# A linear-attention block and a gated mixture of experts on one core: routing steps that read and write PSUM, and another order of the first loads and tables

## Chip, cores and metric

The kernel runs on one core of a Trainium2 chip. The metric is the device time of one execution in microseconds, the median of several runs. Engines are named as in the profile: PE (TensorE), DVE (VectorE), ACT (ScalarE), POOL (GpSimd), SP (the engine that only issues DMAs here); ACT and POOL issue DMAs as well.

## The reference

Linear attention with a state (4 batches, 8 heads, 768 positions, head size 48), and then a mixture of experts with two levels of gates on the 3072 resulting rows of 384 (4 groups of 4 experts, hidden size 1024), all in float32:

```python
for t in range(S):                                  # attention
    cur = einsum('bhd,bhe->bhde', u * k[t], v[t])
    y[t] = einsum('bhd,bhde->bhe', r[t], state + cur)
    state = w * state + einsum('bhd,bhe->bhde', k[t], v[t])
...
g_logits = x @ w_group                              # 4 groups, argmax and softmax weight
e_logits = x @ w_expert[g]                          # 4 experts of that group, the same
out[row] = g_w * e_w * (relu(x[row] @ w1[g, e]) @ w2[g, e])
```

## The kernel before

The positions are cut into 6 chunks of 128, so that there are 24 tiles (chunk, batch). A loop written out by hand over `s` in 0 to 28 (line 510) works on several tiles at once, in this order within a step: `turn(s)` transposes r and k and scales r with a power table (`rT`, line 402; `kT`, copied by ACT, line 404); `own_values(s-1)` (ACT, eight small scalings `dv`); the routing part `choice` if one is due; `rows_T(s-4)` and `row_logits(s-5)` transpose the finished rows and multiply them with the gate weights; `back(s-3)` turns the output back (`xt`, line 471); `values(s-2)` multiplies the masked scores with v (`py`) and updates the state (`pu`, then `R`, lines 455 to 459); `own_sum` (`du`, line 383); the routing parts that are due last; and `scores(s-1)` (`pa`, line 414), which DVE masks into `am` (line 419). The order of each engine's instructions is this program order.

POOL computes `kh` (k times a table, line 373) and `dg` (r times k times u, lines 378 and 379) for pairs of tiles; both multiply 768 elements per partition with both operands in SBUF. It also sends the finished rows to their places in DRAM (`rows`, line 331), with an indirect DMA each.

Routing is done for groups of tiles: five groups of four, then one of two and two of one. `choice` (lines 284 to 297) is due one step after the group's last logits, `gate` and `place` (lines 310 to 327) another step later, `before` ahead of them. All of these are short DVE instructions on tiles in SBUF; the logits are copied from PSUM to `lg` by ACT (line 362). `zero_places` (line 260) clears the rows' places in DRAM in two pieces, from the ACT queue. All PSUM tiles come from one pool of eight banks (line 74).

In the head, `w` is loaded to `w2h` and scanned into powers (`up_to`). Three tables `T1T` (`powers`, line 177) and, turned and flipped by PE and copied by ACT, three tables `T2` (`turned`, line 183) are made from them. `powers(2)`, `turned(0)`, `powers(0)` come ahead of the loop; `later_tables` (line 237) does the rest in step 1. A copy by ACT into `none` (line 156) comes ahead of the scan, and DVE rewrites that column (line 157). All loads of r, k and v (384 KB each) go out on the SP queue; `u` (`ub`), `w` (`wrow`) and the gate weights (`gw`) on the ACT queue.

Behind the loop, the 16 experts run one after the other: `load_rows`, `columns` (transposes), `up` (`ph`, line 632), `down` (`po`, line 645), `rows_out` (line 650). Each expert fills two `px`, four `ph`, three `po` and two `pb` banks.

Of the kernel before, what the change touches and what calls it, by code (L numbers as in the profile page):

```python
# [8 lines left out]
FP32 = mybir.dt.float32  # L9
# [3 lines left out]
OP = mybir.AluOpType  # L13
# [15 lines left out]
def kernel(  # L29
# [43 lines left out]
    wpool = ctx.enter_context(tc.tile_pool(name="wpool", bufs=1))  # L73
    psum = ctx.enter_context(tc.tile_pool(name="psum", bufs=8, space=bass.MemoryType.PSUM))

    def bank(shape, name):
        return psum.tile(shape, FP32, tag="bank", name=name)

    def cst(shape, name, dtype=FP32):
        return const.tile(shape, dtype, name=name)  # L80
# [34 lines left out]

    def load(src, g, dst):
        c, b0 = g // (B // 2), 2 * (g % (B // 2))
        nc.sync.dma_start(
            out=dst.rearrange("p a h d -> p (a h) d"),
            in_=src[b0 : b0 + 2, :, P * c : P * (c + 1), :].rearrange("b h t d -> t (b h) d"),  # L120
        )

    def load_pair(g):

        load(r, g, rts[g % RING][:, :, :, 0:D])
        load(k, g, kts[g % RING])
        load(v, g, vts[g % (RING + 1)][:, :, :, 0:D])

    ub = cst([P, H, D], "ub")
    nc.scalar.dma_start(  # L130
        out=ub.rearrange("p h d -> p (h d)"), in_=bass.AP(tensor=u.tensor, offset=u.offset, ap=[[0, P], [1, H * D]])
    )
    wrow = cst([1, H * D], "wrow")
    nc.scalar.dma_start(out=wrow, in_=bass.AP(tensor=w.tensor, offset=w.offset, ap=[[0, 1], [1, H * D]]))
    load_pair(0)

# [40 lines left out]
    def powers(m):  # L177
        for hc in range(HP):
            nc.vector.tensor_scalar(
                out=T1T[m][:, hc, :], in0=up_to[:, hc, :], scalar1=by[:, m, hc : hc + 1], scalar2=None, op0=OP.mult  # L180
            )

    def turned(m):

        ptab = bank([P, HP, P], "ptab")
        for hc in range(HP):
            nc.tensor.transpose(ptab[:, hc, :], T1T[SPAN - 1 - m][:, hc, :], ident)
        tab = cst([P, HP, P], f"tab_{m}")
        nc.scalar.copy(tab, ptab)
        ptab2 = bank([P, HP, P], "ptab2")  # L190
        nc.tensor.matmul(
            ptab2.rearrange("p a b -> p (a b)"), lhsT=flip, rhs=tab.rearrange("p a b -> p (a b)"), start=True, stop=True
        )
        nc.scalar.copy(  # L194
            T2[m].rearrange("p (a e) d -> p a e d", e=2), ptab2.rearrange("p a (e d) -> p a e d", e=2)[:, :, :, 0:D]
        )
# [4 lines left out]
    nc.vector.tensor_mul(by[:, 0, :], by[:, 0, :], by[:, 1, :])  # L201
    powers(0)


# [31 lines left out]

    def later_tables():
        powers(1)
        turned(1)
        turned(2)  # L240
        nc.vector.tensor_mul(w_span, up_to[:, :, P - 1], up_to[:, :, P - 1])
        nc.vector.tensor_mul(w_span, w_span, up_to[:, :, P - 1])
# [17 lines left out]
    def zero_places(j):  # L260

        regions = xs_dram.rearrange("(e n) w -> n e w", e=GE)
        half = CAP // 2
        nc.scalar.dma_start(out=regions[half * j : half * (j + 1)], in_=spread(nothing[0:half, :], 1, GE))

    def route(pool, lg, xt, T, sums, number, group):

# [5 lines left out]

        NA = 1 + G
        L = lg.rearrange("p i (a e) -> p i a e", e=Eg)
        mx, kx = tl([P, T, NA], "mx"), tl([P, T, NA], "kx")
        key, oh = tl([P, T, NA, Eg], "key"), tl([P, T, NA, Eg], "oh")
        ohe = tl([P, T, G, Eg], "ohe")
        ohf = ohe.rearrange("p i g e -> p i (g e)")
        ex = tl([P, T, NA, Eg], "ex")  # L280
# [3 lines left out]
        def choice():  # L284
            nc.vector.reduce_max(out=mx, in_=L, axis=AX)  # L285

            nc.vector.tensor_tensor(out=key, in0=L, in1=spread(mx, 3, Eg), op=OP.is_ge)
            nc.vector.tensor_mul(
                key.rearrange("p i a e -> p (i a) e"), key.rearrange("p i a e -> p (i a) e"), spread(desc, 1, T * NA)
            )  # L290
            nc.vector.reduce_max(out=kx, in_=key, axis=AX)
            nc.vector.tensor_tensor(out=oh, in0=key, in1=spread(kx, 3, Eg), op=OP.is_equal)
            nc.vector.tensor_mul(ohe, oh[:, :, 1:NA, :], spread(oh[:, :, 0, :], 3, Eg))
            for i in range(T):
                nc.vector.tensor_add(sums[:, i + 1, :], sums[:, i, :], ohf[:, i, :])
            nc.vector.tensor_sub(ex, L, spread(mx, 3, Eg))
            nc.scalar.activation(ex, ex, AF.Exp)
# [12 lines left out]
        def gate():  # L310
            sx = tl([P, T, NA], "sx")
            nc.vector.reduce_sum(out=sx, in_=ex, axis=AX)
            nc.vector.tensor_scalar(out=sx, in0=sx, scalar1=1e-9, scalar2=None, op0=OP.add)
            gg = tl([P, T, G], "gg")
            nc.vector.tensor_mul(gg, sx[:, :, 1:NA], oh[:, :, 0, :])
            se = tl([P, T], "se")
            nc.vector.reduce_sum(out=se, in_=gg, axis=AX)
            nc.vector.tensor_mul(se, se, sx[:, :, 0])
            nc.vector.reciprocal(xt[:, :, DM + ROW_GATE], se)
            nc.vector.tensor_copy(xt[:, :, DM + ROW_ID], number)  # L320

        def place():
            at = tl([P, T, GE], "at")
            nc.vector.tensor_mul(at, held["pre"], ohf)  # L324
            place = tl([P, T], "place")
            nc.vector.reduce_sum(out=place, in_=at, axis=AX)
            nc.vector.tensor_copy(place_i, place)

# [28 lines left out]

    def logits(xT, dst):
        pl = bank([P, NL], "pl")
        for ko in range(KO):  # L360
            nc.tensor.matmul(pl, lhsT=xT[:, ko, :], rhs=gw[:, ko, :], start=(ko == 0), stop=(ko == KO - 1))
        nc.scalar.copy(dst, pl)

# [57 lines left out]
    def values(n):  # L421
# [29 lines left out]
        for e in range(2):  # L451
            rows = slice(DP * e, DP * (e + 1))
            state = R[b][rows, :, DP * e : DP * e + D]
            if c == 0:
                nc.vector.tensor_copy(state, pu[rows])
            else:
                nc.vector.tensor_add(state, pu[rows], state)
            if c % SPAN == SPAN - 1:
                nc.vector.tensor_mul(state, state, spread(w_span[rows, :], 2, D))

    def back(n):

        c, b = tiles[n]
        yT = yTs.pop(n)
        if b == 0:
            xts[c] = pool.tile([P, B, XW], FP32, tag="xt", bufs=3, name="xt")
            lgs[c] = pool.tile([P, B, NL], FP32, tag="lg", bufs=3, name="lg")
        pb = bank([P, HP, 2, DP], "pb")
        for hc in range(HP):
            nc.tensor.transpose(pb[:, hc].rearrange("p e d -> p (e d)"), yT[:, hc, :], ident)  # L470
        nc.vector.tensor_add(
            xts[c][:, b, 0:DM].rearrange("p (h d) -> p h d", h=H), pb.rearrange("p a e d -> p (a e) d")[:, :, 0:D],
            dvs.pop((n // 2, n % 2)),
        )
# [5 lines left out]

    def row_logits(n):
        c, b = tiles[n]
        logits(xTs.pop(n), lgs[c][:, b, :])


    ROUTED = {B * c + B - 1: B for c in range(NCH - 1)}
    ROUTED.update({NT - 3: 2, NT - 2: 1, NT - 1: 1})

    def routing(n):
        T = ROUTED[n]  # L490
        c, b = tiles[n]
        first = n + 1 - T
        b0 = b + 1 - T
        return route(
            rpool, lgs[c][:, b0 : b + 1, :], xts[c][:, b0 : b + 1, :], T, cum[:, first : n + 2, :],
            tok[:, c, b0 : b + 1], "rows to places",
        )
# [3 lines left out]
    scale_k(0, nc.gpsimd, 1, 2)  # L501
    for t in rts[1:] + khs[1:] + vts[1:]:
        nc.gpsimd.memset(t[:, :, :, D:DP], 0.0)
    load_small()
    load_pair(1)
    own(0)
# [3 lines left out]
    for s in range(NT + LAST):  # L510
# [11 lines left out]
        if s % 2 == 0 and s // 2 + 2 < NP:  # L522
            load_pair(s // 2 + 2)
        if s in (3, 6):
            zero_places(s // 6)
        if s == 18:
            early[0] = load_expert(0, wpool)
        run("first")
        if s < NT:
            turn(s)  # L530
            if s % 2 == 1 and s // 2 + 1 < NP:
                scale_k(s // 2 + 1, nc.gpsimd)
                own(s // 2 + 1)
# [12 lines left out]
        if s % 2 == 0 and s // 2 < NP:  # L546
            own_sum(s // 2)
        if s == 1:
            later_tables()
        run("last")  # L550
# [143 lines left out]
    with tc.If(more > 0, preferred_fallthrough_block=False):  # L694
        with tc.tile_pool(name="rest", bufs=1) as rest:
# [5 lines left out]
            with tc.If(ok < 1):  # L701
                with tc.tile_pool(name="scan", bufs=1) as sc:
# [54 lines left out]
                    with tc.For_i(0, NT, 1) as i:  # L757
# [4 lines left out]
                        )  # L762
                        lr = sc.tile([P, 1, NL], FP32, name="lr")
                        xT = sc.tile([P, KO, P], FP32, name="xT")
                        transposed(xr[:, 0, 0:DM], xT)
                        logits(xT, lr[:, 0, :])
                        again = route(sc, lr, xr, 1, cum[:, 0:2, :], number, "rows to places again")
                        for part in again[0:4]:
# [136 lines left out]
```

## Time and profile before

| | us |
|---|---|
| median of 3 runs | 560.56 (559.77 to 562.12) |
| profiled execution | 556.86, its span 555.0 |
| PE busy | 490.2 (88%) |
| DVE busy | 192.0 (35%) |
| ACT busy | 139.5 (25%) |
| POOL busy | 125.0 (23%) |

The profile is of one execution. Busy shares are means over the attention part (up to about 226 us) and the experts (from 233 us), which have different limits, so that they are read by stage. [...]

### The profile page before, as it was taken

The numbers are of one execution on the slowest core, as the hardware profiler recorded it, in microseconds if no ns is written. First come the engines' busy times: TensorE is split into PE (matmuls) and PEld (weight loads), VectorE is DVE, ScalarE is ACT, GpSimd is POOL, SyncE is SP. The second block draws the span as 40 slices with busy tenths as digits, with TensorE's granted clock in tenths as the row PEclk, the third lists the DMA queues.
The fourth block names the chain that finished last, engine by engine and source line by source line (L and its number), as shares of the span: only waits on it lengthen the run. The fifth ranks groups of instructions, "written<-read, shape, count | busy, mean of one in ns | idle before, by whom it ended". The sixth has DMA issues, their size and how long they took to land. (4 is left out here: it accounts for less than half of the span.)

```text
span 555.0 us, 8734 instructions
## 1 busy us (share of the span) xinstructions
PE 490.2 (88%) x3533; PEld 468.9 (84%) x3533; DVE 192.0 (35%) x491; ACT 139.5 (25%) x416; POOL 125.0 (23%) x115
## 2 busy tenths in 40 slices
PE   4388988978988995399999999999999999999993
PEld 2168887877877884399999999999999999999992
DVE  4567676786765957201011101001110100101000
ACT  2244544342443542011111111111111111111110
POOL 3853432354524423201011001101100110110011
PEclk9697997777977996599999999999999999999998
DMA  9999993264800055534565647456564756555000
GB/s 146 161 175 292 278 137 57 60 114 86 272 14 30 31 172 170 157 111 163 202 211 163 226 165 244 163 200 214 156 230 164 236 169 199 186 160 202 24 25 24
DMA packets 110589, 85.88 MB, mean 155 GB/s; under 512 B 78451, under 2 KB 102137, under 8 KB 110542
## 3 DMA queue, kind: packets, MB, share of 16 engines
q1 hardware_dynamic: 97356, 64.49, 45.8%
q10 hardware_dynamic: 9858, 11.30, 6.4%
q0 software_dynamic: 3328, 9.47, 4.8%
q8 instruction: 29, 0.48, 0.4%
q14 instruction: 18, 0.15, 0.1%
HBM read 70.25 MB, written 15.78 MB: 155 GB/s over the span
## 5 line engine op out<-in xcount | busy, mean ns | idle before, releaser
L632 PE MATMUL ph<-xe,w 128*128 128x224 f32 x768 | 152.0, 355 | 1.3 <-issue 1.3
L645 PE MATMUL po<-hT,w 128*128 128x224 f32 x768 | 150.7, 353 | 0.0
L632 PEld LDWEIGHTS ph<-xe,w 128*128 128x128 f32 x768 | 145.3, 192 | 1.9 <-issue 1.6
L645 PEld LDWEIGHTS po<-hT,w 128*128 128x128 f32 x768 | 144.1, 190 | 0.0
L662 POOL DMA_INDIRECT out_dram<-yt,ids x32 | 30.6, 955 | 292.0 <-DVE yt L657 287.2
L657 DVE TENSOR_SCALAR yt<-pb,gates 128x384 f32<-128x384 f32 (+1 forms) x32 | 18.2, 611 | 167.0 <-PE pb L655 167.0
L636 ACT ACTIVATE hT<-ph 128x448 f32<-128x448 f32 x64 | 34.8, 544 | 136.9 <-PE ph L632 136.9
L648 ACT COPY yT<-po 128x224 f32<-128x224 f32 x48 | 16.6, 346 | 134.7 <-PE po L645 99.0
L389 ACT ACTIVATE dv<-vt,du 128x48 f32<-128x48 f32 x192 | 45.9, 324 | 5.2 <-DVE du L383 5.2
L378 POOL TENSOR_TENSOR dg<-rt,kt 128x768 f32<-128x768 f32 x12 | 22.0, 1829 | 80.4 <-DVE du L383 80.4
L613 DVE COPY xe<-px 128x448 f32<-128x448 f32 (+1 forms) x32 | 14.7, 503 | 65.5 <-PE px L610 65.5
L436 PE MATMUL py<-am,vt 128*64 128x128 f32 x384 | 32.6, 314 | 3.8 <-DVE am L419 3.8
L419 DVE TENSOR_TENSOR am<-pa,later 128x512 f32<-128x512 f32 x48 | 30.9, 686 | 13.6 <-PE pa L414 9.7
L436 PEld LDWEIGHTS py<-am,vt 128*64 128x64 f32 x384 | 25.4, 158 | 8.5 <-DVE am L419 5.5
L331 POOL DMA_INDIRECT x_sorted<-xt,place_i x24 | 23.8, 994 | 32.2 <-DVE mx L285 16.9
L430 PE MATMUL py<-rT,R 128*128 128x128 f32 x160 | 25.7, 313 | 5.3 <-DVE at L324 5.3
L414 PE MATMUL pa<-rT,kT 48*128 48x128 f32 x384 | 29.5, 296 | 0.0
L430 PEld LDWEIGHTS py<-rT,R 128*128 128x128 f32 x160 | 23.6, 227 | 5.8 <-DVE at L324 5.8
L414 PEld LDWEIGHTS pa<-rT,kT 48*128 48x128 f32 x384 | 24.8, 198 | 2.5 <-issue 1.3
L404 ACT COPY kT<-pk 128x512 f32<-128x512 f32 x24 | 14.0, 586 | 45.8 <-PE pk L400 39.8
L373 POOL TENSOR_TENSOR kh<-kt,T 128x768 f32<-128x768 f32 (+1 forms) x12 | 21.5, 1791 | 16.2 <-ACT T L194 9.7
L441 ACT COPY yT<-py 128x512 f32<-128x512 f32 x24 | 14.1, 587 | 33.6 <-PE py L436 31.1
(109 smaller groups left out, 443.9 us busy)
## 6 DMA issues: line engine op xcount, KB each, us to landing
w<-in_moe_w_dram SPq DMA_DIRECT2D x32, 1536.0 KB, 6.4
x_sorted<-nothing ACTq DMA_DIRECT2D x2, 2702.0 KB
rt<-in_r_dram SPq DMA_DIRECT2D x12, 384.0 KB, 7.0
kt<-in_k_dram SPq DMA_DIRECT2D x12, 384.0 KB, 7.0
vt<-in_v_dram SPq DMA_DIRECT2D x12, 384.0 KB, 10.8
xg<-x_sorted ACTq DMA_DIRECT2D x16, 193.0 KB, 2.5
xg<-x_sorted ACTq DMA_DIRECT2D x16, 144.8 KB, 3.3
out_dram<-yt,ids POOLq DMA_INDIRECT x32, 2.4
```

Source lines behind the costliest of these rows:

```text
L331: ins = nc.gpsimd.indirect_dma_start(out=xs_dram, out_offset=bass.IndirectOffsetOnAxis(ap=place_i[:, i : i + 1], axis=0), in_=xt[:, i, :], ...
L373: engine.tensor_mul(khs[g % (RING - 1)][:, a0:a1, :, 0:D], kts[g % RING][:, a0:a1], spread(T2[m], 1, a1 - a0))
L378: nc.gpsimd.tensor_mul(dg, rts[g % RING][:, :, :, 0:D], kts[g % RING])
L389: nc.scalar.mul(dv[:, h, :], vts[g % (RING + 1)][:, a, h, 0:D], dvs[g][:, a, h : h + 1])
L414: nc.tensor.matmul(pa[e][:, hc, :], lhsT=kT[rows, hc, :], rhs=rT[rows, hc, :], start=True, stop=True, skip_group_check=True,)
L419: nc.vector.tensor_mul(am[:, e], pa[e], spread(later, 1, HP))
L430: nc.tensor.matmul(py[:, hc, :], lhsT=R[b][:, hc, :], rhs=rT[:, hc, :], start=(hc == 0), stop=False, skip_group_check=True,)
L436: nc.tensor.matmul(py[DP * e : DP * (e + 1), hc, :], lhsT=vt[:, a, 2 * hc + e, :], rhs=am[:, e, hc, :], start=(c == 0), stop=True, skip_gr ...
L632: nc.tensor.matmul(ph[:, i, :], lhsT=w1[:, ko, P * (f + i) : P * (f + i + 1)], rhs=xe[:, ko, :], start=(ko == 0), stop=(ko == KO - 1), ski ...
L636: nc.scalar.activation(hTs[e][:, f : f + 2, :], ph, AF.Relu)
L645: nc.tensor.matmul(po, lhsT=w2[:, fo, P * d : P * (d + 1)], rhs=hT[:, fo, :], start=(fo == 0), stop=(fo == FO - 1))
L662: ins = nc.gpsimd.indirect_dma_start(out=out, out_offset=bass.IndirectOffsetOnAxis(ap=ids, axis=0), in_=yt, in_offset=None, bounds_check=N ...
```

## The change

Routing (`choice`, `gate`, `place`) works on a PSUM bank of its own: `row_logits` writes the logits of all tiles of a group into one bank, from where they are read without a copy, and the intermediate tiles alternate so that each DVE instruction has at most one operand in SBUF (where it read two). `oh` is split into `ohg` and `ohx`; `ohp` is a second copy of `ohe` in PSUM; the addition of 1e-9 is fused into the next instruction; the copy of the row numbers goes to ACT. The state decay at every third chunk adds in PSUM and multiplies from there. Two of the eight banks go to routing. In the head, pairs 0 and 1 are loaded before `u` and `w`, their k on the ACT queue; the memsets of `rts[1]` and `vts[1]` go from POOL to DVE; all power tables are computed ahead of the loop, the flips of tables 1 and 2 follow `turn(0)`; `span_decay` moves from step 1 to 2. The zeroing of the places goes out in four pieces in steps 3, 5, 7 and 9.

```diff
-    psum = ctx.enter_context(tc.tile_pool(name="psum", bufs=8, space=bass.MemoryType.PSUM))
+    psum = ctx.enter_context(tc.tile_pool(name="psum", bufs=6, space=bass.MemoryType.PSUM))
+    rpsum = ctx.enter_context(tc.tile_pool(name="rpsum", bufs=2, space=bass.MemoryType.PSUM))
...
-    def load_pair(g):
+    def load_pair(g, k_queue=nc.sync):
         load(r, g, rts[g % RING][:, :, :, 0:D])
-        load(k, g, kts[g % RING])
+        load(k, g, kts[g % RING], k_queue)
         load(v, g, vts[g % (RING + 1)][:, :, :, 0:D])
     ub = cst([P, H, D], "ub")
+    wrow = cst([1, H * D], "wrow")
+    load_pair(0, nc.scalar)
     nc.scalar.dma_start(out=ub...)
-    wrow = cst([1, H * D], "wrow")
+    nc.vector.memset(rts[1][:, :, :, D:DP], 0.0)
+    nc.vector.memset(vts[1][:, :, :, D:DP], 0.0)
+    load_pair(1, nc.scalar)
     nc.scalar.dma_start(out=wrow, ...)
-    load_pair(0)
...
     powers(0)
+    flipped(0)
+    powers(1)
+    turned(1)
+    turned(2)
...
-        half = CAP // 2
-        nc.scalar.dma_start(out=regions[half * j : half * (j + 1)], in_=spread(nothing[0:half, :], 1, GE))
+        part = CAP // 4
+        nc.scalar.dma_start(out=regions[part * j : part * (j + 1)], in_=spread(nothing[0:part, :], 1, GE))
...
-        L = lg.rearrange("p i (a e) -> p i a e", e=Eg)
+        L = part(NL, "p (i a e) -> p i a e", e=Eg)
+        key = part(NL, "p (i a e) -> p i a e", e=Eg)
+        ohx = part(GE, "p (i g e) -> p i g e", e=Eg)
+        ohp = part(GE, "p (i g e) -> p i g e", e=Eg)
+        sx = part(NA, "p (i a) -> p i a")
+        se = part(1, "p (i a) -> p i a")
+        ohg = tl([P, T, Eg], "ohg")
+        place_f = part(1, "p (i a) -> p i a")
...
-            nc.vector.tensor_tensor(out=oh, in0=key, in1=spread(kx, 3, Eg), op=OP.is_equal)
-            nc.vector.tensor_mul(ohe, oh[:, :, 1:NA, :], spread(oh[:, :, 0, :], 3, Eg))
+            nc.vector.tensor_tensor(out=ohg, in0=key[:, :, 0, :], in1=spread(kx[:, :, 0], 2, Eg), op=OP.is_equal)
+            nc.vector.tensor_tensor(out=ohx, in0=key[:, :, 1:NA, :], in1=spread(kx[:, :, 1:NA], 3, Eg), op=OP.is_equal)
+            nc.vector.tensor_mul(ohe, ohx, spread(ohg, 3, Eg))
+            nc.vector.tensor_mul(ohp, ohx, spread(ohg, 3, Eg))
             for i in range(T):
-                nc.vector.tensor_add(sums[:, i + 1, :], sums[:, i, :], ohf[:, i, :])
+                nc.vector.tensor_add(sums[:, i + 1, :], sums[:, i, :], ohp[:, i].rearrange("p g e -> p (g e)"))
...
-            nc.vector.tensor_scalar(out=sx, in0=sx, scalar1=1e-9, scalar2=None, op0=OP.add)
-            nc.vector.tensor_mul(gg, sx[:, :, 1:NA], oh[:, :, 0, :])
+            nc.vector.scalar_tensor_tensor(out=gg, in0=sx[:, :, 1:NA], scalar=1e-9, in1=ohg, op0=OP.add, op1=OP.mult)
-            nc.vector.tensor_mul(se, se, sx[:, :, 0])
+            nc.vector.scalar_tensor_tensor(out=se, in0=sx[:, :, 0:1], scalar=1e-9, in1=ge, op0=OP.add, op1=OP.mult)
-            nc.vector.tensor_copy(xt[:, :, DM + ROW_ID], number)
+            nc.scalar.copy(xt[:, :, DM + ROW_ID], number)
...
-            if c % SPAN == SPAN - 1:
-                nc.vector.tensor_mul(state, state, spread(w_span[rows, :], 2, D))
+            elif c % SPAN < SPAN - 1:
+                nc.vector.tensor_add(state, pu[rows], state)
+            else:
+                nc.vector.tensor_add(pu[rows], pu[rows], state)
+                nc.vector.tensor_mul(state, pu[rows], spread(w_span[rows, :], 2, D))
...
-    for t in rts[1:] + khs[1:] + vts[1:]:
+    for t in khs[1:] + rts[2:] + vts[2:]:
         nc.gpsimd.memset(t[:, :, :, D:DP], 0.0)
     load_small()
-    load_pair(1)
...
-        if s in (3, 6):
-            zero_places(s // 6)
+        if s in (3, 5, 7, 9):
+            zero_places(s // 2 - 1)
...
             turn(s)
+            if s == 0:
+                flipped(1)
+                flipped(2)
...
-        if s == 1:
-            later_tables()
+        if s == 2:
+            span_decay()
```

## Rows read from the trace of the kernel before

**Rows 1.** Busy by stage: PE, PEld, DVE, ACT, POOL, clock, DMA share, GB/s.

```profile
204.78:226.10 21.32, 11.75 (x83) 10.55 (x83) 14.73 (x85) 2.97 (x12) 7.83 (x8) 0.68 0.40 139
...
233.34:547.60 314.26, 312.32 (x1722) 310.05 (x1722) 38.27 (x121) 51.46 (x112) 29.65 (x31) 1.00 0.50 170
```

**Rows 2.** The page's slices: granted TensorE clock in tenths, 40 equal slices.

```profile
PEclk9697997777977996599999999999999999999998
```

**Rows 3.** Busy time by step, same columns; three sums over three steps first.

```profile
74.10:104.30 30.20, 24.82 (x239) 22.96 (x238) 22.46 (x45) 10.42 (x37) 13.06 (x8) 0.77 0.56 92
110.74:139.43 28.69, 22.54 (x224) 20.86 (x224) 21.35 (x42) 10.07 (x37) 14.11 (x10) 0.76 0.57 97
145.97:175.44 29.47, 24.01 (x231) 22.36 (x230) 20.66 (x40) 10.43 (x37) 14.79 (x10) 0.77 0.22 78
...
67.56:74.10 6.54, 6.54 (x84) 6.25 (x85) 4.11 (x8) 3.42 (x12) 0.80 (x1) 1.00 1.10 162
...
82.55:97.26 14.71, 11.86 (x103) 11.27 (x101) 9.27 (x20) 6.33 (x24) 3.65 (x2) 0.74 0.37 54
...
181.97:189.15 7.18, 6.58 (x83) 6.01 (x81) 6.82 (x18) 3.49 (x13) 5.66 (x4) 1.00 0.13 49
189.15:194.20 5.05, 5.05 (x60) 4.64 (x59) 4.79 (x15) 3.52 (x13) 0.00 (x0) 1.00 0.04 13
```

**Rows 4.** Timeline of a choice: start us, us, engine, line, operation [idle before <-releaser].

```profile
76.05 1.82 POOL L379 TENSOR_TENSOR dg<-dg,ub 128x768 f32<-128x768 f32 x1
76.16 1.80 DVE L287 TENSOR_TENSOR key<-lg,mx 128x80 f32<-128x80 f32 x1
```

**Rows 5.** Timeline of a gate.

```profile
92.63 1.82 POOL L378 TENSOR_TENSOR dg<-rt,kt 128x768 f32<-128x768 f32 x1 [12.55 <-DVE du L383]
92.72 1.76 DVE L313 TENSOR_SCALAR sx<-sx 128x20 f32<-128x20 f32 x1
```

**Rows 6.** By tile: ns min/median/max, first and last start, forms.

```profile
L402 DVE TENSOR_TENSOR rT<-pr,T1T x24: 669/681/684, 11.4 to 195.4; 128x512 f32<-128x512 f32 x24
L287 DVE TENSOR_TENSOR key<-lg,mx x8: 178/1017/1828, 76.2 to 220.5; 128x80 f32<-128x80 f32 x5, 128x20 f32<-128x20 f32 x2, 128x40 f32<-128x40 f32 x1
```

**Rows 7.** Timeline: an undisturbed choice, then an undisturbed gate and place.

```profile
205.99 0.23 DVE L285 TENSOR_REDUCE mx<-lg 128x20 f32<-128x80 f32 x1
...
208.33 0.23 DVE L296 TENSOR_TENSOR ex<-lg,mx 128x80 f32<-128x80 f32 x1
...
192.39 0.23 DVE L312 TENSOR_REDUCE sx<-ex 128x20 f32<-128x80 f32 x1
...
194.12 0.17 DVE L327 CAST place_i<-place 128x4 uint32<-128x4 f32 x1
```

**Rows 8.** Groups by line and shape: count | busy us, mean ns | idle before.

```profile
L293 DVE TENSOR_TENSOR ohe<-oh 128x64 f32<-128x64 f32 x5 | 1.1, 224 | 0.2
L324 DVE TENSOR_TENSOR at<-pre,ohe 128x64 f32<-128x64 f32 x5 | 1.1, 222 | 0.0
```

**Rows 9.** Timeline of the first 36 us.

```profile
1.21 0.53 ACTq L134 DMA_DIRECT2D wrow<-in_w_dram  x1
...
2.43 1.90 SPq L118 DMA_DIRECT2D kt<-in_k_dram  x1
...
3.32 0.06 DVE L157 MEMSET none<- 128x1 f32 x1 [1.17 <-ACT none L156]
...
18.33 0.95 DVE L383 TENSOR_REDUCE du<-dg 128x16 f32<-128x768 f32 x1 [6.22 <-POOL dg L379]
...
19.80 4.02 DVE L179 TENSOR_SCALAR T1T<-up_to,by 128x128 f32<-128x128 f32 x4
20.12 1.85 POOL L373 TENSOR_TENSOR kh<-kt,T 128x768 f32<-128x768 f32 x1
...
29.68 1.16 PE L414 MATMUL pa<-rT,kT 48*128 48x128 f32 x16
...
34.62 0.95 DVE L383 TENSOR_REDUCE du<-dg 128x16 f32<-128x768 f32 x1
```

## What the trace lets one predict

> **What bounds the kernel now.** I read busy times by stage first, then the page's slices, then busy times by step, and the timeline of the steps that stand out. The program has three parts. The expert loop is a wall of matmuls: 312.3 of 314.3 us busy at a clock of 1.00 [rows 1], so it gives nothing and can only lose. The tail before it (21.3 us) is a chain of small routing instructions, VectorE busy for 14.7 us in 85 pieces [rows 1]. The attention part before that is uneven: the slices of the granted clock there fall to 6 and 7 tenths again and again [rows 2].
>
> By steps (cut at the start of each tile's mask multiply `am`) the unevenness has a place. A step without routing takes 6.54 us and TensorE is busy in all of it at clock 1.00. The two steps that carry a group's `choice` and its `gate`/`place`, with the step behind them, take 30.20, 28.69 and 29.47 us for the first three groups, at a mean clock of 0.76 to 0.77; the gate step alone takes 14.71 us at 0.74 [rows 3]. The fourth group is the natural experiment: its choice step takes 7.18 us and its gate step 5.05 us, both at 1.00 [rows 3].
>
> What differs is GpSimd. The 80-element `key` compare starts 0.11 us after a GpSimd multiply (76.05, 1.82 us) and ends with it: 1.80 us [rows 4]. `sx` in the gate does the same beside 92.63: 1.76 us [rows 5]. Over all groups `key` runs from 178 to 1828 ns, while `rT`, which reads one operand from PSUM, stays at 669 to 684 ns in all its 24 runs [rows 6], though it too runs beside GpSimd. In a group undisturbed by GpSimd the choice takes 2.5 us (205.99 to the end of `ex`), and gate plus place 1.8 us (192.39 to the end of the cast) [rows 7]. [...]
>
> **Routing with one operand in PSUM.** Removed: all two-SBUF-operand steps of choice, gate and place, and the SBUF `tensor_scalar` (+1e-9), hence their holds. Added in choice: two instructions (`oh` becomes `ohg` and `ohx`; `ohp` repeats `ohe`), 0.2 to 0.25 us each by `ohe` [rows 8]. Removed in gate: one by fusing the 1e-9, one by the id copy that moves to ScalarE, about 0.3 us. Choice becomes 2.5 + 0.5 = 3.0 us, gate plus place 1.5 us. Both are shorter than in the fourth group, where the clock held although its `key` was still held by 1.6 us (2.5 + 1.6 = 4.1), so I price groups 1 to 3 as steps of its kind: 7.2 (choice) + 5.05 plus 0.7 (an estimate, a tenth of a step) for the state update that it no longer had (gate) + 6.5 (the step behind) = 19.5, and I take 20.3 for the decay multiplies in group 1 and small waits. Sum: 3 x 20.3 = 61 against 88.4 now [rows 3]: -27 us. The fourth group gives at most 0.5.
>
> What VectorE pays to *write* PSUM no row shows. Reading costs nothing: 64 elements take 222 ns from PSUM (`at`) and 224 ns from SBUF (`ohe`) [rows 8]. Lower bound 0 by that; upper bound another 0.15 us per instruction, about a whole short instruction. I take 0, since the nearest row shows none; at the upper end the choice becomes 5 us, longer than the fourth group's, and the clock may fall again (second rival).
>
> [...]
>
> **Logits left in their bank.** 24 ScalarE copies of `lg` go; ScalarE isn't late there, so 0, and a few tenths in the tail where the first routing step waits for one.
>
> **Six banks instead of eight.** A step fills eight banks (nine before) plus `pre`. With six, `pa` waits for `rT` and `kT` of its own step and `py` for the previous `am`, which it needs anyhow; I find no new wait on the path in a plain step: 0. What covers it is that each bank is emptied within a few fills; if `pre` keeps one for a whole gate step, five are left, and I allow 1 us per group. In the experts some 11 banks are filled per expert in 314.3 / 16 = 19.6 us, so a bank comes round again after about 11 us, where emptying takes under one: 0.
>
> **Tail.** Each group has two instructions more in choice and two fewer in gate. They trade evenly; the last group of four pays 0.5 in its choice ahead of the chain. I take +1 (0 to +6, if some 40 PSUM writes cost 0.15 each).
>
> **Head: tables first, loads on two queues.** Today VectorE waits 6.2 us in `du` for GpSimd's `dg`; only then does it compute the third power table, beside GpSimd's `kh`, in 4.0 us; the table transposes stand in TensorE's queue ahead of the first scores, which start at 29.7 [rows 9]. After the change the powers are computed while GpSimd is idle, and the scores no longer wait behind them. Next in line is GpSimd's own chain (`kh`, memsets, `dg`, state memset, `kh` of pair 1, `dg` of pair 1). It starts at the first table (two short memsets go from it to VectorE; I leave them out). `kh` of pair 1 ends at 21.97 now, so 21.97 plus any delay D of the first table; two multiplies of 1.85 later `du` of pair 1 runs at 25.7 + D, against 34.62 now [rows 9]. That is -8.9 + D.
>
> D comes from the ScalarE queue. Two 384 KB loads, the `u` load and `w` now stand in front of the small copy into `none`, and VectorE's scan waits for that copy (it already waits 1.17) [rows 9]. Now the queue is through at 1.74. A load behind a big one takes 1.90 to issue [rows 9]. Lower bound of D: two more issues of 0.5 as `wrow`, 1.0. Upper bound: all four take 1.9, which is 0.8 + 7.6 - 1.74 = 6.7. I take that `u` and `w` each wait 1.9 behind a big one and the big ones go in at 0.4: 0.8 + 4.6 - 1.74 = 3.7. Eight more table transposes on TensorE, two table copies and the five `gw` issues on ScalarE now come before the first `kT`; they hide under the GpSimd chain, which is later (if it weren't, they would cost a few us each). Head: -8.9 + 3.7 = -5.2, bounds -7.9 and -2.2; I take -5. The loads themselves gain nothing, and the zero fill in four pieces is over a choice and a gate step before the first row is sent: 0, or a wait of POOL's row writes if the fourth piece is late.
>
> **Sum.** -27 - 5 + 1 = -31. The profiled execution took 556.9 us, 555.0 of them span; that gives 525.9 for it. The median of the runs is 560.56, 3.7 above the profiled one, so the median forecast is 560.56 - 31 = 529.6, say 530.
>
> **Rivals.**
> *The clock still falls.* The holds go, but the choice with PSUM writes still idles TensorE enough to halve the clock in the gate step, as in the first three groups. Then only the hold time is saved: two holds in choice and two in gate, each 1.55 us as in [rows 4, 5], 6.2 per group, less the added instructions 5.4, so 16 in three groups; with head and tail 560.56 - 20 = 541. For: three of four groups fall today. Against: the fourth, with one hold in its choice, does not [rows 3].
> *Fewer banks or dear PSUM writes eat half.* TensorE waits some 0.5 us in most of 24 steps and the tail takes +5: about -13, 548.
> *The change doesn't do what it says.* VectorE is held whatever one operand does. Then only the head remains: 556.6. The 24 even `rT` [rows 6] speak against.
> *Slower: the experts run out of banks.* If with six banks TensorE loses time in each expert, the price is 1.8 us per bank filling, 16 times, 29 us: 558.5 at one per expert, which about cancels the gain; beyond 1.9 us per expert the kernel is slower; at two fillings 587. It decides if a bank is held for longer than five fillings. Against: nothing but 2 us of idle TensorE in the loop [rows 1].
>
> **How the numbers follow.** Forecast 530 (522 to 537) 0.66; clock still falls, 541, 0.14; half eaten, 548, 0.07; not as it says, 556.6, 0.04; experts slower, 587, 0.04; better than 521 (head at its bound, fourth group and early steps gaining too) 0.05. The range of 8 in 10 takes in the forecast and the second case: 521 to 545. A measurement of this kernel tells about 0.5% (2.8 us) from no change. Faster by more than that: 0.66 + 0.14 + 0.07 + 0.05 and half of the fourth case, about 0.93; within it 0.03; slower 0.04.
>
> **What would show it.** `key`, `sx`, `se` and `cum` even and short beside running GpSimd multiplies; clock 1.00 from the sixth tile to the tail; choice and gate steps near 7 and 6; `du` of pair 1 near 29; the expert loop still 314 us without TensorE waits. The prediction is wrong if the gate steps still show 0.74, if the scan in the head starts after 11 us (or at 5), or if waits of TensorE on `xt`, `at` or `yT` appear in plain steps.

## The result, and the profile after

The changed kernel takes 520.64 us (median of 4 runs, 519.88 to 521.87) against 560.16 (559.09 to 562.12) of the kernel before, measured beside it: a ratio of 0.929, 95% interval 0.926 to 0.933. Its profiled execution took 519.9 us, 518.1 of them span. The forecast was 530, with a range of 521 to 545: the direction came true and so, in the main, did the reasons; the gain was 39.5 us instead of 30.6, and the time lies 0.4 us below the range.

The slices of the granted clock, to be laid beside [rows 2]: the 6 and 7 tenths of the attention part are gone. The 8 tenths of the second and third slice are the head, and what is left of 5 to 7 tenths is the tail. The granted clock is a share of full speed. In the trace of the kernel before it stands at 0.50 from 20 to 26, 84 to 87, 98 to 102 and 120 to 125 us and at 1.00 from 55 to 80; numbers between are means over a stretch.

```profile
PEclk9889999999999657999999999999999999999997
```

Busy time by stretch (length, then PE, PEld, DVE, ACT, POOL busy with counts, clock, DMA share, GB/s). First the choice step, the gate step and the step behind it of the first three groups, as the sums in [rows 3]; then the tail, and the experts' loop, as [rows 1]:

```profile
68.21:88.81 20.60, 19.30 (x236) 17.62 (x235) 15.53 (x44) 10.30 (x35) 10.96 (x7) 1.00 0.93 193
95.62:113.70 18.08, 17.30 (x223) 15.93 (x223) 14.62 (x42) 9.90 (x35) 12.46 (x9) 1.00 0.61 133
120.24:137.99 17.75, 17.69 (x231) 16.73 (x230) 13.88 (x40) 10.30 (x35) 12.35 (x9) 1.00 0.36 132
165.70:195.10 29.40, 14.19 (x89) 12.20 (x89) 16.20 (x93) 3.00 (x12) 7.81 (x8) 0.63 0.44 143
...
195.10:509.90 314.80, 313.57 (x1722) 311.07 (x1722) 38.33 (x121) 51.45 (x112) 29.07 (x31) 0.99 0.50 169
```

The three sums fall from 30.20, 28.69 and 29.47 to 20.60, 18.08 and 17.75 us, all at clock 1.00. The cleanest reading puts one stretch of the same work side by side: from the mask multiply of the eighth tile to that of the last, TensorE runs 1188 matmuls in both kernels. First before, then after:

```profile
74.10:204.78 130.68, 112.69 (x1188) 104.61 (x1187) 93.32 (x188) 54.76 (x195) 52.47 (x36) 0.84 0.42 98
```

```profile
68.21:165.70 97.49, 95.28 (x1188) 88.78 (x1187) 71.45 (x189) 54.00 (x183) 52.63 (x36) 1.00 0.57 151
```

The stretch is 33.2 us shorter. TensorE's idle time (length less busy) falls from 18.0 to 2.2 us, which is 15.8; the same matmuls take 95.3 instead of 112.7 us, which is 17.4 more and is the clock. So here each microsecond of idle TensorE was paid about once more by matmuls at the lower clock. DVE's busy time falls by 21.9 us at nearly the same count of instructions: that is the holds. In the kernel before, `key`, `cum`, `sx`, `se`, `oh` and the decays (`R`, line 459) together take 22 us more in this stretch than the same instructions take undisturbed.

A choice and the gate of the same group, in the order of time (start us, us, engine, line, operation, what ended the idle time before it). `rb` is the routing bank:

```profile
70.16 1.82 POOL L406 TENSOR_TENSOR dg<-dg,ub 128x768 f32<-128x768 f32 x1
70.28 0.25 DVE L315 TENSOR_TENSOR rb<-rb,mx 128x80 f32<-128x80 f32 x1
70.56 0.25 DVE L316 TENSOR_TENSOR rb<-rb,desc 128x80 f32<-128x80 f32 x1
...
72.69 0.23 DVE L326 TENSOR_TENSOR ex<-rb,mx 128x80 f32<-128x80 f32 x1
...
82.70 0.24 DVE L341 TENSOR_REDUCE rb<-ex 128x20 f32<-128x80 f32 x1
82.75 1.83 POOL L405 TENSOR_TENSOR dg<-rt,kt 128x768 f32<-128x768 f32 x1 [8.55 <-DVE du L410]
82.98 0.17 DVE L343 SCALAR_TENSOR_TENSOR gg<-rb,ohg 128x16 f32<-128x16 f32 x1
...
84.19 0.16 DVE L356 CAST place_i<-rb 128x4 uint32<-128x4 f32 x1
```

The `key` compare (line 315) starts 0.12 us after a GpSimd multiply, as in [rows 4], and takes 0.25 us instead of 1.80. The choice takes 2.9 us (from `mx` at 70.01 to the end of `ex`), gate and place 1.65, both beside GpSimd at work.

The head, as [rows 9] (ACTq is ScalarE's DMA queue):

```profile
0.80 0.43 ACTq L120 DMA_DIRECT2D kt<-in_k_dram  x1
1.26 1.45 ACTq L134 DMA_DIRECT2D ub<-in_u_dram  x1
2.73 0.46 ACTq L120 DMA_DIRECT2D kt<-in_k_dram  x1
3.22 3.09 ACTq L140 DMA_DIRECT2D wrow<-in_w_dram  x1
6.34 1.28 ACT L161 ACT_TABLE_LOAD   x1 [6.34 <-issue]
7.63 0.19 ACT L161 COPY none<-ones 128x1 f32<-128x1 f32 x1
...
8.06 1.37 DVE L175 TENSOR_TENSOR_SCAN up_to<-wc,none 128x128 f32<-128x128 f32 x4
...
11.07 1.66 DVE L184 TENSOR_SCALAR T1T<-up_to,by 128x128 f32<-128x128 f32 x8
...
14.75 1.36 POOL L400 TENSOR_TENSOR kh<-kt,T 128x384 f32<-128x384 f32 x1 [10.89 <-ACT T L204]
...
21.58 0.95 DVE L410 TENSOR_REDUCE du<-dg 128x16 f32<-128x768 f32 x1 [4.23 <-POOL dg L406]
...
29.97 0.95 DVE L410 TENSOR_REDUCE du<-dg 128x16 f32<-128x768 f32 x1
```

The kernel before, for comparison:

```profile
3.06 0.19 ACT L156 COPY none<-ones 128x1 f32<-128x1 f32 x1
...
4.11 0.16 DVE L166 TENSOR_SCALAR wc<-pw 128x4 f32<-128x4 f32 x1 [0.73 <-PE pw L164]
4.30 1.37 DVE L170 TENSOR_TENSOR_SCAN up_to<-wc,none 128x128 f32<-128x128 f32 x4
...
23.93 1.71 DVE L242 TENSOR_TENSOR w_span<-w_span,up_to 128x4 f32<-128x4 f32 x1
```

The scan starts at 8.06 us instead of 4.30, because a table load and the copy stand behind four DMA issues on ScalarE. Before, the copy was done at 3.25, and what the scan then waited for was `wc`, which comes from the loaded w by way of TensorE (4.11). The eight pieces of T1T are no longer held (0.21 us each instead of 1.0), and `du` of the second pair runs at 29.97 instead of 34.62.

Where the 36.9 us of span come from, by the start of `am` of each tile: -5.9 up to the eighth tile; -31.9 in the three groups; +0.4 in the plain step behind the first; -1.6 in the fourth group and the two steps behind it; +0.8 in the tail (29.40 us to the first matmul of the experts; the 21.32 of [rows 1] end earlier, and to that matmul, at 233.34, it was 28.56); +1.3 in the experts and behind them. The last comes with the first expert, which starts with a clock of 0.86 in its first 20.2 us (0.92 before); the two rows of the experts' loop differ by less, since they don't end equally far behind the last matmul.

### The profile page after: what moved, and what is told of

The parts are those of the page before. It is cut to its first block, busy times and chain, and to the rows that moved or that the text cites. A ratio compares the mean times of both kernels' runs of the same rounds, so it can differ in the third digit from the quotient of the medians.

```text
span 518.1 us, 8753 instructions
## 1 busy us (share of the span) xinstructions
PE 472.7 (91%) x3533; PEld 454.6 (88%) x3533; DVE 165.1 (32%) x493; ACT 138.1 (27%) x400; POOL 124.7 (24%) x113
## 3 DMA queue, kind: packets, MB, share of 16 engines
q1 hardware_dynamic: 93228, 63.71, 41.9%
## 5 line engine op out<-in xcount | busy, mean ns | idle before, releaser
L694 POOL DMA_INDIRECT out_dram<-yt,ids x32 | 30.6, 956 | 293.4 <-DVE yt L689 288.5
L463 PE MATMUL py<-am,vt 128*64 128x128 f32 x384 | 28.3, 285 | 1.8 <-DVE am L446 1.7
L463 PEld LDWEIGHTS py<-am,vt 128*64 128x64 f32 x384 | 21.9, 140 | 5.6 <-DVE am L446 2.5
L406 POOL TENSOR_TENSOR dg<-dg,ub 128x768 f32<-128x768 f32 x12 | 21.8, 1819 | 0.9
L457 PE MATMUL py<-rT,R 128*128 128x128 f32 x160 | 21.3, 276 | 0.4 <-DVE at L354 0.4
L389 PEld LDWEIGHTS rb<-gw,xT 128*128 128x128 f32 x144 | 19.2, 203 | 2.9 <-issue 2.9
```

Source lines behind the costliest of these rows:

```text
L406: nc.gpsimd.tensor_mul(dg, dg, spread(ub, 1, 2))
L463: nc.tensor.matmul(py[DP * e : DP * (e + 1), hc, :], lhsT=vt[:, a, 2 * hc + e, :], rhs=am[:, e, hc, :], start=(c == 0), stop=True, skip_gr ...
L694: ins = nc.gpsimd.indirect_dma_start(out=out, out_offset=bass.IndirectOffsetOnAxis(ap=ids, axis=0), in_=yt, in_offset=None, bounds_check=N ...
```

## Experiments

Two theories stand behind the 27 us forecast for the groups. *Holds and clock*: VectorE is held while GpSimd reads SBUF, TensorE idles for it, and then runs the next step at half clock. The rival, *holds alone*: only the held time itself is saved. All experiments are read by the stretch of 1188 matmuls above, too (eighth tile to last), since its idle part and its clock part can be told apart.

### Routing alone, and the head alone

The first is the changed kernel with the loads, power tables, memsets and zeroing of before; the second is the kernel before with those of the change.

```diff
-    load_pair(0, nc.scalar)
...
-    load_pair(1, nc.scalar)
...
+    load_pair(0)
...
-    powers(1)
-    turned(1)
-    turned(2)
...
+        if s == 1:
+            later_tables()
```

> The changed kernel with the head, the table order, the loads and the zeroing of before: routing in PSUM and six banks alone. Theory H+C (a held VectorE costs its hold and then the fall of the clock behind it): the three groups give 31.9 us as in the trace of after, the fourth and fifth 1.6, the tail takes 1 to 2: 560 - 32 = 528. Rival H (only the holds count, 5.4 us per group; the rest of the gain is the head's): 560 - 16 - 2 = 542.

> The kernel before with the new loads, table order and zeroing alone, routing in SBUF and eight banks. Theory H+C: only the lead at the eighth tile counts, 5.9 us: 554. Rival H: the head gives what routing does not, some 22 us: 538. If the two parts add up, e1 and e2 together lose 39.5 us.

Routing alone took 526.52 us (ratio 0.940, 0.936 to 0.943), the head alone 552.42 (0.985, 0.982 to 0.987), with 560.45 for the kernel before beside them. Both lie near the first theory's 528 and 554. That is -33.9 and -8.0: together 41.9, a little more than the 39.5 of both. The spans of the profiled executions give -31.5 and -4.3, together 35.8 of 36.9; part of the -8.0 is that the median of the kernel before stands above its profiled execution. The stretch, routing alone first:

```profile
75.70:171.90 96.20, 94.69 (x1188) 88.43 (x1187) 71.34 (x189) 54.00 (x183) 52.60 (x36) 1.00 0.48 133
```

```profile
67.20:199.90 132.70, 114.28 (x1188) 106.58 (x1186) 93.34 (x188) 54.70 (x195) 52.43 (x36) 0.83 0.54 119
```

Routing does all of the stretch, the head nothing in it: of the 6.9 us that the head wins up to the eighth tile (67.2 instead of 74.1), 2.0 are lost again in the stretch. With routing alone that tile comes at 75.7, 1.6 us later than before: up to there the new routing with its six general banks costs something and gives nothing. The decay that adds in PSUM and the zeroing in four pieces were not tried by themselves.

### Only the gate, and only the choice, in SBUF again

The changed kernel, with gate and place on SBUF tiles, and then with the choice on SBUF tiles (logits copied by ACT).

```diff
-            nc.vector.reduce_sum(out=sx, in_=ex, axis=AX)
+            sxs = tl([P, T, NA], "sxs")
+            nc.vector.reduce_sum(out=sxs, in_=ex, axis=AX)
+            nc.vector.tensor_scalar(out=sxs, in0=sxs, scalar1=1e-9, scalar2=None, op0=OP.add)
...
+            nc.vector.tensor_mul(ses, ses, sxs[:, :, 0])
...
```

```diff
-        L = part(NL, "p (i a e) -> p i a e", e=Eg)
-        key = part(NL, "p (i a e) -> p i a e", e=Eg)
+        LP = part(NL, "p (i a e) -> p i a e", e=Eg)
+        key, L = tl([P, T, NA, Eg], "keys"), tl([P, T, NA, Eg], "lgs")
...
+            nc.scalar.copy(L, LP)
```

> The changed kernel with gate and place back in SBUF (with the separate addition of 1e-9 and the id copy on VectorE); choice stays in PSUM. Holds come back in the gate steps of three groups, 3.1 us each. Rival H: 3 x 3.1 = +9, about 530. Theory H+C: each hold idles TensorE and one to two steps behind it run at the half clock, +2 to 3 more per group: +16, about 537, with a mean granted clock clearly under 1.00 in the steps behind the gates only.

> The changed kernel with choice in SBUF (one copy of the logits per group on ScalarE, key, ohx, ohp and the logits in SBUF); gate and place stay in PSUM. Holds come back in four choices, 1.5 to 4 us each. Rival H: +3.5 per group, +11 to +14, about 533. Theory H+C: the gate step behind each held choice runs at a clock of about 0.75 as before and takes some 5 us more: 3 x 8 = +24, about 545.

Gate in SBUF: 535.47 us (0.955, 0.952 to 0.959), 15 us above the change and near the 537 of the first theory. Choice in SBUF: 540.54 (0.964, 0.959 to 0.969), 20 above. The holds are back, one behind the other, in the gate of the second group of the first kernel:

```profile
113.74 1.81 POOL L406 TENSOR_TENSOR dg<-rt,kt 128x768 f32<-128x768 f32 x1 [4.51 <-DVE du L411]
113.84 1.75 DVE L343 TENSOR_SCALAR sxs<-sxs 128x20 f32<-128x20 f32 x1
...
115.63 1.83 POOL L407 TENSOR_TENSOR dg<-dg,ub 128x768 f32<-128x768 f32 x1
...
116.03 1.45 DVE L348 TENSOR_TENSOR ses<-ses,sxs 128x4 f32<-128x4 f32 x1
```

Its gate steps are 3.1 to 3.2 us longer than the change's. The steps behind them, where nothing is held, are 1.6, 2.6 and 1.3 us longer in the three groups, at clocks of 0.56, 0.57 and 0.73. The first row below is that of the second group; in the change the same 61 matmuls take 3.99 us. In the choice experiment the lower clock falls on the gate step behind the choice (second row, 7.41 us in the change):

```profile
118.30:124.90 6.60, 6.60 (x61) 6.16 (x61) 3.10 (x7) 0.58 (x1) 3.19 (x3) 0.57 0.30 79
```

```profile
111.40:122.80 11.40, 11.39 (x96) 10.89 (x95) 5.47 (x16) 4.59 (x16) 1.52 (x1) 0.67 0.04 8
```

TensorE is busy in all of both steps, so what they lose can't be a wait: it is the clock. The stretch takes 112.9 us in the first (11.4 idle, 101.5 busy) and 118.5 in the second (13.3 idle, 105.3 busy). Against the change's 97.5 that is 15.4, of which 9.2 idle and 6.2 clock, and 21.0, of which 11.0 idle and 10.0 clock. Holds and clock are both there; holds alone would leave out the second figure of each. The time of the choice experiment lay between the two expectations; its clock part decides it. (Its choice also waits for the copy of the logits, 0.25 us in the second group, which is no hold.)

### Does GpSimd hold VectorE by working, or by reading?

The kernel before, routing in SBUF as it was; the two multiplies that make `dg` become five memsets of the same tile.

```diff
-        nc.gpsimd.tensor_mul(dg, rts[g % RING][:, :, :, 0:D], kts[g % RING])
-        nc.gpsimd.tensor_mul(dg, dg, spread(ub, 1, 2))
+        for i in range(5):
+            nc.gpsimd.memset(dg, 0.0)
```

> The kernel before with the two 768-element multiplies that make dg (1.82 us each) replaced by five GpSimd memsets of the same tile (about 0.75 us each, so about the same 3.7 us of GpSimd): the term with u is left out of the computation, the kh multiplies stay. Theory 1, GpSimd holds VectorE because it reads SBUF: no key, ohe or cum beside a memset is longer than 0.35 us; holds stay only beside kh. Half to three quarters of the lost time in groups 1 to 3 goes: 535 to 548. The sx (tensor_scalar with SBUF in and out) may still be held beside a memset, for at most 0.75 us. Theory 2, any busy GpSimd holds it: key beside a memset ends with the memset, and the time stays above 552.

It took 526.7 us (0.941, 0.938 to 0.944), lower than either theory said. In order of time: a choice, a gate, and a state decay beside the `kh` multiply that stayed:

```profile
72.42 3.92 POOL L379 MEMSET dg<- 128x768 f32 x5 [5.76 <-DVE du L383]
...
74.45 0.24 DVE L287 TENSOR_TENSOR key<-lg,mx 128x80 f32<-128x80 f32 x1
...
85.38 3.92 POOL L379 MEMSET dg<- 128x768 f32 x5 [6.93 <-DVE du L383]
85.50 0.65 DVE L313 TENSOR_SCALAR sx<-sx 128x20 f32<-128x20 f32 x1
...
92.00 2.07 DVE L459 TENSOR_TENSOR R<-R,w_span 64x192 f32<-64x192 f32 x1
92.01 1.83 POOL L373 TENSOR_TENSOR kh<-kt,T 128x768 f32<-128x768 f32 x1
```

Beside a GpSimd that only writes, `key` with its two SBUF operands takes 0.24 us; beside `kh`, which reads, a decay is held for 2.07. `sx`, a `tensor_scalar` from SBUF to SBUF, is held to the end of one memset (0.65). So in these rows it is the reading (and, for that one form, the writing) and not the work as such. With the same routing as before, the stretch falls from 130.7 to 101.8 us, that is 28.9 of the change's 33.2. I had taken the remaining `kh` holds for a quarter to a half of the loss; all that remains, 4.3 us of 33.2, is an eighth.

### How many banks are enough?

The kernel before with six banks instead of eight and nothing else; then the changed kernel with five instead of six (and its two routing banks).

```diff
-    psum = ctx.enter_context(tc.tile_pool(name="psum", bufs=8, space=bass.MemoryType.PSUM))
+    psum = ctx.enter_context(tc.tile_pool(name="psum", bufs=6, space=bass.MemoryType.PSUM))
```

```diff
-    psum = ctx.enter_context(tc.tile_pool(name="psum", bufs=6, space=bass.MemoryType.PSUM))
+    psum = ctx.enter_context(tc.tile_pool(name="psum", bufs=5, space=bass.MemoryType.PSUM))
```

> The kernel before with six PSUM banks instead of eight and nothing else. My theory: banks come free in time in the steps and in the experts: 560, within 0.5%. Rival (banks bind): TensorE waits on its readers, at least 1.8 us per expert or 0.5 us per step, 570 or more.

> The changed kernel with its general pool cut from six banks to five (routing keeps its two). In the kernel before, going from eight to six cost 13 us, all of it around the routing steps. Theory 1: the banks were dear there because choice and gate held them for long; in the changed kernel choice takes 2.9 us and gate with place 1.65 us, so that a bank fewer costs under 3 us: 521 to 524. Theory 2: six banks are already the edge for TensorE, and a step short of a bank costs as much as in the kernel before, about 6.5 us or more per bank: 527 or slower. Either way the expert loop stays within 1 us, since a bank comes round there after eight fillings or so.

Here my view fell twice. Six banks cost the kernel before 14.8 us (573.67 against 558.9; ratio 1.028, 1.024 to 1.033), and five cost the changed kernel 17 (537.68; 0.960, 0.956 to 0.963). TensorE's longest waits in the stretch, before with six (what waited, for what, us in all, times, longest):

```profile
PE pa L414 <- DVE xt L471: 12.2, 3, 4.6
PE pl L361 <- DVE at L324: 7.4, 2, 3.7
PE pb L470 <- DVE at L324: 3.2, 1, 3.2
```

And with eight:

```profile
PE pr L400 <- DVE xt L471: 5.6, 3, 2.6
```

The stretch takes 142.8 us instead of 130.7, which is 12.1 of the 16.7 us by which the span grows. Another 3.9 are lost ahead of it (the eighth tile comes at 77.95 instead of 74.10), where no choice or gate has run yet; so not all of it lies around the routing steps, as I had assumed in the second expectation. With six banks the scores and the logits of a routing step wait until `xt` or `at`, which stand in VectorE's queue behind the held choice and gate, have emptied a bank; with eight such a step had two banks to go on with, and TensorE's longest waits for `xt` come later, at `pr`. The change shortens exactly those steps, and takes the logits out of the pool, so that its own waits in the stretch are 1.9 us in all:

```profile
PE pre L331 <- DVE xt L498: 0.8, 1, 0.8
PE pa L441 <- DVE xt L498: 0.7, 1, 0.7
PE py L457 <- DVE at L354: 0.4, 1, 0.4
```

But six is the edge. With five, nothing is held and DVE's busy time is the same (71.5 us), and the stretch takes 110.8:

```profile
73.50:184.30 110.80, 100.75 (x1189) 92.20 (x1188) 71.52 (x190) 53.96 (x183) 52.45 (x36) 0.97 0.47 126
```

That is 13.3 more than the change: 7.8 of it idle, 5.5 longer matmuls. The clock explains some 3.3 of the 5.5 (an estimate: 0.03 of 110.8 us; it reads 0.92 from 106.0 to 128.6); what the rest is stays open. The experts don't mind in either kernel (314.9 us with six banks in the kernel before). Whether a seventh bank would bring the change anything wasn't tried: with the two routing banks that would make nine, and the kernel before has eight in all.

### The head once more

In the changed kernel the copy with its table load, and GpSimd's memsets, stand on the head's chain. First the copy ahead of ScalarE's loads; then GpSimd's memsets (11 of them, `R` too) ahead of its first multiply; then both, with `span_decay` and the late constants ahead of the loop, before GpSimd starts to read (the test of w's limits goes to step 0).

```diff
     nc.sync.dma_start(out=w2h[:, :, 0:D], in_=w.rearrange("(a e) d -> a e d", e=2))
+    ones = cst([P, P], "ones")
+    nc.vector.memset(ones, 1.0)
+    none = cst([P, P], "none")
+    nc.vector.memset(none, 0.0)
+    nc.scalar.copy(none[:, 0:1], ones[:, 0:1])
...
```

```diff
     numbers()
+    for t in khs[1:] + rts[2:] + vts[2:]:
+        nc.gpsimd.memset(t[:, :, :, D:DP], 0.0)
+    for t in R:
+        nc.gpsimd.memset(t, 0.0)
     scale_k(0, nc.vector, 0, 1)
...
```

```diff
     numbers()
+    span_decay()
+    late_constants()
...
```

> The changed kernel with the small ScalarE copy into none (and the load of its table) ahead of ScalarE's DMAs instead of behind them. Theory (the delay D of 3.76 us in the scan carries through the GpSimd chain to the end): -3.5, about 517. Rival (the loads or TensorE's tables are next, because the k loads now start 1.5 us later): 0 to -1, about 520.

> The changed kernel with GpSimd's 11 memsets (seven paddings and the four states, 3.9 us) ahead of its first multiply, in the time in which it waits for the first table. Theory (GpSimd's chain sets the head): kh of pair 1 and du of pair 1 come 3.9 us earlier and the kernel gains 3 to 4: 517. Rival (TensorE's tables and the first scores set it): about 520.

> e6 and e7 together, and span_decay and the small constants computed right behind the third power table, the check of w while VectorE waits for the first dg. Theory: 3.5 + 3.5 and some 2 to 3 us of VectorE time in step 2: 511 to 514. Rival (the chain moves to the loads, which are at the DMA's rate): no better than the best of e6 and e7 by more than 1 us, 516.

They took 518.2 us (0.927, 0.923 to 0.931), 516.94 (0.925, 0.921 to 0.928) and 508.54 (0.909, 0.905 to 0.913), beside 558.9 for the kernel before. Each of the first two brings the last tile's mask multiply from 165.7 to 163.1 us in its trace; by their ratios alone neither can be told from the change with certainty. Both together, with the constants, bring it to 155.3, which is more than the sum, and the time is below the 511 to 514 expected; the rival that had the loads next is out (the DMA share of the change is 1.10 over its first 26 us). What the constants alone are worth was not tried. Rows of the third kernel:

```profile
2.09 0.19 ACT L118 COPY none<-ones 128x1 f32<-128x1 f32 x1
...
4.17 1.95 POOL L535 MEMSET R<- 128x512 f32 x4
...
4.72 1.37 DVE L174 TENSOR_TENSOR_SCAN up_to<-wc,none 128x128 f32<-128x128 f32 x4
...
9.49 0.17 DVE L252 TENSOR_TENSOR w_span<-w_span,up_to 128x4 f32<-128x4 f32 x1
...
17.71 0.93 DVE L410 TENSOR_REDUCE du<-dg 128x16 f32<-128x768 f32 x1
...
23.06 0.95 DVE L410 TENSOR_REDUCE du<-dg 128x16 f32<-128x768 f32 x1
```

The scan is back at 4.72, GpSimd fills its idle start with the memsets, and `du` of the second pair runs at 23.06 instead of 29.97. `w_span`, a two-operand multiply of four elements, takes 0.17 us here; in the change it was held for 1.82 by the `dg` multiply beside it, and before for 1.71 (23.93 above). This kernel is faster than both, with an interval well clear of the change's.

## Where the prediction was right, and where it failed

**The mechanism: right.** The choice holds and the gate holds each idle TensorE, and behind each runs a step at a lower clock: in the stretch 18.0 us of idle TensorE and a clock of 0.84 before, 11.4 and 0.92 with the gate holds alone, 13.3 and 0.90 with the choice holds alone, 2.2 and 1.00 after. The rival on which the clock still falls (541) is out: no slice between the head and the tail shows it. The gate and choice experiments give the two parts apart.

**The three groups: the step that failed.** I put 7.2 (choice) + 5.75 (gate) + 6.5 (the step behind) = 19.5 and took 20.3. The steps measured are 6.2 + 9.8 + 4.5, 6.7 + 7.4 + 4.0 and 5.9 + 7.9 + 4.0: 20.6, 18.1 and 17.75, in all 56.4 instead of 61, which is 4.6 us (4.9 with the rounding of the 27). The mechanism held; the size of this term did not. The choice step was priced as the fourth group's 7.18 [rows 3], although I had said in the same sentence that this one still held a `key` for 1.6 us. Without the hold it is 5.6, and 5.9 to 6.7 were measured: that is 2.9 us of the 4.6. Most of the rest is the allowance of 0.8 per group for decays and small waits. Gate and step behind together take 14.4, 11.4 and 11.9 us, where 12.25 stood: the first group, in which two of the four tiles with a decay fall, used more than its allowance, the other two none. (That the decays are the reason is argued, no run shows it.) How 12.25 was split, 5.75 for the gate and 6.5 for a plain step behind it, was wrong as well, but cancels: since gate and place stand ahead of `am` on VectorE, a longer gate only pushes the cut between the two steps, and TensorE has that much less left in the step behind. A small misreading had no effect: the undisturbed gate and place of [rows 7] take 1.9 us, not 1.8.

**The fourth group** and the steps behind it gave 1.6, where I said at most 0.5 and left it out of the sum: 1.0 in its own steps, as its choice lost its hold, and 0.6 behind them.

**The head: right in its chain, and near in its number by luck.** D, the delay of the first table, was put at 3.7 from the issue times; 3.76 were measured, but two errors cancel in it. The two big loads went in at 0.43 and 0.46 and the loads behind them took 1.45 and 3.09, 4.5 in all, where I had 1.9 each; so the copy came 4.57 us later (7.63 instead of 3.06). And the scan of before did not wait for that copy, as I had read (the 1.17 of [rows 9] is the wait of the memset), but for `wc`, and started 0.8 us later than the copy and the memset required. The same holds for the sum: 5.9 us were won up to the eighth tile instead of 5, but the new order alone is worth 6.9 (the head alone, 74.1 to 67.2) to 7.5 (75.7 with routing alone to 68.2 with both), and 1.0 to 1.6 went to the new routing and its six banks, which I had put at 0 there. The memsets and the table copy that I left on that chain turned out to be worth 12 us more, together with the late constants (the last experiments): the chain I had named, GpSimd's, was the right one, but I asked only what the change does to it, not what stood on it needlessly.

**PSUM writes: right.** I took 0 between 0 and 0.15 us per instruction. The 80-element `key` takes 0.25 us from PSUM to PSUM (70.28 in the kernel after), 0.24 from SBUF to SBUF where it isn't held (74.45, beside the memsets).

**Six banks: right for the change, for a reason that was wrong.** I argued that a bank is emptied within a few fills, whatever the routing does. The kernel before with six banks shows that this isn't so (14.8 us). In the stretch it holds in the change because the held steps are gone (ahead of it something is lost, as said under the head), and one bank fewer would already cost 17 us: the margin that I described wasn't there. The rival that put the loss into the experts had the wrong place.

**Tail and experts:** +0.8 and +1.3 against +1 and 0.

**From the trace to the median.** The forecast for the profiled execution was 525.9, and it took 519.9: 6.0 of the 9 us by which the median missed are the terms above (4.9 in three groups, 1.6 in and behind the fourth, 0.9 in the head, 0.2 in the tail, less 1.3 in the experts and 0.4 in a plain step). The other 3 us come from the last line of the sum: I added the 3.7 us by which the median stood above the profiled execution of before, and after it the median stands only 0.7 above. Such a gap belongs to single executions and isn't carried over; it should have widened the range downwards by as much, which would have held the time.

## What to carry to other kernels

A small VectorE instruction with two operands in SBUF cost as much here as the GpSimd instruction that it met (`key` 1.80 us beside a multiply of 1.82 [rows 4]). One operand in PSUM (0.25 us), or a GpSimd that only wrote at that moment (0.24), freed it, and what this was worth is the hold, and, where TensorE waited for it and then ran at the lower clock, more again: for each microsecond of idle TensorE 0.7 to 1.1 here (6.2 to 9.2, 10.0 to 11.0 and 17.4 to 15.8 us). Price a step by rows of a step that has lost what yours will lose, and read two neighbouring steps together if the cut between them is set by the engine that the change speeds up. Before taking banks from a pool, take one more away on the kernel that keeps them: the waits show where the edge is.

## What the runs showed of the hardware that was not expected

- A 0.19 us copy on ScalarE brought a table load of 1.28 us with it, and both stood behind four DMA issues that took 5.5 us on its queue (0.80 to 6.31). The `u` load took 1.45 and the `w` load 3.09 us to issue behind 384 KB loads, where `wrow` took 0.53 with no big load ahead of it [rows 9].
- A `tensor_scalar` from SBUF to SBUF was held beside a GpSimd memset, which only writes (0.65 us, to the memset's end, against 0.18 undisturbed); a two-operand `key` beside the same kind of memset was not (0.24).
- One PSUM bank fewer lost 7.8 us of TensorE's time to waits in 110.8, in 14 waits of at most 1.4 us where the change has 3, and its matmuls took 5.5 us longer, some 3.3 of it by the clock (0.97 on average).
